# ScalarE's order at the ends of the passes, and the last output tile in two halves, in a kernel of banded attention and a mixture of experts

## The chip, the cores and the metric

The kernel runs on one core of a Trainium2 chip. The metric is the device time of one execution in microseconds (us); the lower the better. The engines of the core are named as in the profile: PE is TensorE's matmuls, PEld its loads of weights, DVE is VectorE, ACT is ScalarE, POOL is GpSimd, SP is SyncE, which issues the DMAs.

## The reference

Attention with a local band and a few global keys makes `x` (3072 rows of 512). Eight experts follow, each a layer of 512 to 1024 with a ReLU and a layer of 1024 to 512, weighted by a matrix `P` of a Sinkhorn iteration, all in float32:

```python
attn_out = _attn_ref(**attn_kwargs)
B, H, S, D = attn_out.shape
x = np.ascontiguousarray(attn_out.transpose(0, 2, 1, 3)).reshape(B * S, H * D)
...
for e in range(E):
    h = np.maximum(x @ w1[e], 0.0)
    ye = h @ w2[e]
    out += P[:, e:e + 1] * ye
```

## The kernel before

**Numbers in two parts.** A float32 operand is held as a high and a low part (`wh` and `wl`, `w2h` and `w2l`, `hh` and `hl`), and each product is three matmuls: high times low, low times high, high times high. The high part of a weight is a cast on ScalarE, the low part a subtraction on GpSimd (`split`, L605 and L606). A matmul therefore waits for both.

**Passes and groups.** After the attention (the first 270 us or so), the 3072 rows are worked on in three blocks of 1024. For each block one pass runs over the weights, in 31 groups of 256 columns of an expert's hidden layer. One group is one step of the loop in `pipeline`:

- Layer one (`layer1_strassen`) by Strassen's scheme: seven products m1 to m7, of six matmuls each, in the order m3, m2, m1, m6, m5, m4, m7, into four banks of PSUM, named c, d, a, b. m3 reads a part of `wh` and `wl` that comes straight from the weights (`w1f`); m2, the second product, reads a part that comes from sums of weights (`wsum`, made on GpSimd, L628). The banks are combined on DVE (L718 to L732; the copy at L716 is the first step), and each is then evicted: ReLU on ACT (L677), then the low part on DVE (L678), into one of two sets of `h` in turn (their names are `h_set` and `x`). When DVE reads a bank, ACT's eviction of that bank waits for this read.
- Layer two (`second`, `layer2`): eight tiles of 128 rows, six matmuls each into a tile `y_ps`, which DVE then adds to the accumulators (L1041, L1045; the buffer is named `early`).

Layer two runs one step behind: layer one of group n, then layer two of group n - 1. At the end of a pass (`p > 0 and g % NG == 0`) both layers two are done before the next pass, so that layer one of the new pass's first two groups follow each other without a layer two between them.

**Weights.** `strassen_stage` loads `w1f` and `w2f` of a group and makes `wsum`; the staging buffers are single. `strassen_pair` makes the high and low parts in this order of the code: the two small ones from `w1f`, then `w2h` from `w2f`, then the big one of five blocks from `wsum`. The results lie in one of two pools, in turn, each with a single buffer: the parts of group n + 2 overwrite those of group n. `w2h` of group n + 2 thus waits until layer two of group n has ended on PE.

**What sets the order.** A scheduler places the instructions on their engines and may put a later one first, except those that are given to `keep_in_program_order`, which stand among themselves in the order of the code. The class `Ordered` wraps an engine in this way. All matmuls of the main loop are kept in order (`moe.pe = attention.pe` once an expert above 0 is reached). `moe.act` is the ScalarE handle for casts and ReLUs: it is wrapped in `Ordered` for the last unit of the attention, and is the bare engine in the main loop, so that the scheduler places casts and evictions there.

**The end.** The last group of a pass also stores each finished tile of the output, 128 rows of 512 columns, from SP's queue (L1048).

## Time and profile before

| what | us |
|---|---|
| runs (3): median, least, most | 2182.03, 2181.88, 2183.47 |
| the profiled execution | 2182.23 |
| its span, from the first instruction to the last | 2180.3 |
| TensorE busy in the span | 2166.7 |
| mean granted TensorE clock, of full speed | 0.999 |

The page of a profile shows one execution. A row of the timeline gives the start in us from the span's start, the length, the engine, the line of the kernel, the operation with output and input, and in brackets the idle time of the engine before it with what ended it. Where a line is that of a wrapper (L110 for all ordered matmuls, L54 for what `Ordered` wraps), the tile's name tells what the instruction is. The chain of waits follows the end of the program back, at each step to what released it. Numbers at the end of a tile's name tell buffers apart in the program's order; the profile leaves them out.

### The profile page before, as it was taken

Reading aid. Unit: us, or ns where it says so; the run is one execution under the profiler, and the core shown is the slowest. Engines: PE = TensorE matmul, PEld = TensorE weight load, DVE = VectorE, ACT = ScalarE, POOL = GpSimd, SP = SyncE. Lnnn points to the kernel's source line nnn. Section 1 sums busy time; section 2 is a strip of 40 time slices with the busy share of each in tenths; the row PEclk is TensorE's granted clock in tenths of the full one; section 3 lists DMA queues with packets and bytes.
Section 4 is the critical chain, followed back from the end, with each engine's and each line's share of the span. In section 5 each row is a group of like instructions: output and inputs, shape, how many; then the busy total and the mean of one; then the engine's idle time right before and its main releaser. Section 6 shows DMA issues by size and latency. Waiting matters only on the chain.

```text
span 2180.3 us, 29188 instructions
## 1 busy us (share of the span) xinstructions
PE 2166.7 (99%) x10785; PEld 1797.7 (82%) x10785; DVE 1375.7 (63%) x2422; ACT 747.4 (34%) x1513; POOL 1153.8 (53%) x1076
## 2 busy tenths in 40 slices
PE   8999999999999999999999999999999999999998
PEld 6888888888888888888888888888888888888887
DVE  7777577566566566566566566566566566566565
ACT  7777633222222232232222232232242232222221
POOL 5977865455454454455454454454455455454440
PEclk9999999999999999999999999999999999999999
DMA  6777531111111111711111111113411111111111
GB/s 164 211 210 205 166 141 58 49 49 59 49 49 58 49 49 59 260 49 58 49 49 58 49 49 58 49 49 127 135 49 58 49 49 58 49 49 58 49 39 51
DMA packets 207881, 175.57 MB, mean 81 GB/s; under 512 B 101232, under 2 KB 170352, under 8 KB 207728
## 3 DMA queue, kind: packets, MB, share of 16 engines
q1 hardware_dynamic: 207728, 173.60, 25.6%
q8 instruction: 87, 1.43, 0.3%
q14 instruction: 66, 0.54, 0.1%
HBM read 144.46 MB, written 29.10 MB: 80 GB/s over the span
## 4 chain that ended last, share of the span: by engine, by line
PE 98%; DVE 1%; DMA 1%; ACT 1%; issue 0%; SPq 0%; DVEq 0%; ACTq 0%
PE y_ps L110 46%; PE bank_a L110 11%; PE bank_d L110 11%; PE bank_c L110 11%; PE bank_b L110 6%; PE t_ps L113 2%; PE o_ps L110 2%; PE s_ps L110 2%; PE h_ps L110 1%; PE tp L113 1%; PE y_ps L748 1%; PE y_ps L746 1%; PE y_ps L747 1%; PE g_ps L110 0%; PE r_ps L113 0%; DMA raw_q<-in_q_dram 0%
## 5 line engine op out<-in xcount | busy, mean ns | idle before, releaser
L1045 DVE SCALAR_TENSOR_TENSOR early<-y_ps,pm,early 128x512 f32<-128x512 f32 x672 | 503.7, 750 | 243.9 <-PE y_ps L110 242.8
L110 PE MATMUL y_ps<-w2h,h_set 128*128 128x512 f32 x1440 | 443.3, 389 | 0.0
L110 PE MATMUL y_ps<-w2h,x 128*128 128x512 f32 x1440 | 443.3, 389 | 0.0
L606 POOL TENSOR_TENSOR wl<-w1f,wh 128x256 fp32r<-128x256 f32 x186 | 134.1, 740 | 561.3 <-ACT wh L605 560.3
L606 POOL TENSOR_TENSOR w2l<-w2f,w2h 128x1024 fp32r<-128x1024 f32 x93 | 222.5, 2393 | 292.7 <-ACT w2h L605 292.7
L628 POOL TENSOR_TENSOR wsum<-w1f 128x256 f32<-128x256 f32 x465 | 327.7, 739 | 84.0 <-DMA w1f<-in_moe_w_dram 84.0
L605 ACT CAST w2h<-w2f 128x1024 fp32r<-128x1024 f32 x92 | 96.9, 1053 | 717.6 <-issue 636.5
L110 PEld LDWEIGHTS y_ps<-w2h,h_set 128*128 128x128 f32 x1440 | 270.3, 188 | 56.1
L110 PEld LDWEIGHTS y_ps<-w2h,x 128*128 128x128 f32 x1440 | 270.3, 188 | 56.1
L110 PE MATMUL y_ps<-w2l,x 128*128 128x512 f32 x720 | 280.1, 389 | 0.0
L110 PE MATMUL y_ps<-w2l,h_set 128*128 128x512 f32 x720 | 280.1, 389 | 0.0
L606 POOL TENSOR_TENSOR wl<-wsum,wh 128x1280 fp32r<-128x1280 f32 x93 | 274.8, 2955 | 3.1
L110 PE MATMUL bank_a<-m,wh 128*128 128x512 f32 x712 | 248.3, 389 | 0.9 <-DVE h_set L678 0.5
L110 PE MATMUL bank_d<-x,wh 128*128 128x512 f32 x712 | 248.2, 389 | 0.0
L110 PE MATMUL bank_c<-x,wh 128*128 128x512 f32 x712 | 248.1, 389 | 0.0
L718 DVE TENSOR_TENSOR early<-early,bank_d 128x512 f32<-128x512 f32 x93 | 64.0, 688 | 187.3 <-PE bank_d L110 177.6
L110 PEld LDWEIGHTS y_ps<-w2l,x 128*128 128x128 f32 x720 | 135.1, 188 | 28.1
L110 PEld LDWEIGHTS y_ps<-w2l,h_set 128*128 128x128 f32 x720 | 135.1, 188 | 28.0
L110 PEld LDWEIGHTS bank_a<-m,wh 128*128 128x128 f32 x712 | 133.6, 188 | 29.5 <-DVE x L678 0.9
L110 PEld LDWEIGHTS bank_c<-x,wh 128*128 128x128 f32 x712 | 133.6, 188 | 27.8
L110 PEld LDWEIGHTS bank_d<-x,wh 128*128 128x128 f32 x712 | 133.6, 188 | 27.7
L110 PE MATMUL bank_a<-m,wl 128*128 128x512 f32 x356 | 138.5, 389 | 0.0
(235 smaller groups left out, 3406.2 us busy)
## 6 DMA issues: line engine op xcount, KB each, us to landing
w1f<-in_moe_w_dram SPq DMA_DIRECT2D x94, 512.0 KB, 3.4
w2f<-in_moe_w_dram SPq DMA_DIRECT2D x94, 512.0 KB, 3.4
x<-op_m SPq DMA_DIRECT2D x16, 512.0 KB, 7.1
op_m<-op SPq DMA_DIRECT2D x30, 256.0 KB, 2.7
m<-op_m SPq DMA_DIRECT2D x12, 512.0 KB, 8.7
out_dram<-early SPq DMA_DIRECT2D x24, 256.0 KB, 4.0
ys<-y_sb SPq DMA_DIRECT2D x21, 256.0 KB, 2.7
early<-ys SPq DMA_DIRECT2D x21, 256.0 KB, 4.5
```

Source lines behind the costliest of these rows:

```text
L110: return self.tc.keep_in_program_order(self.engine.matmul(*args, **kw))
L113: return self.tc.keep_in_program_order(self.engine.transpose(*args, **kw))
L605: self.act.copy(out=hi, in_=full)
L606: self.nc.gpsimd.tensor_tensor(out=lo, in0=full, in1=hi, op=ALU.subtract)
L628: nc.gpsimd.tensor_tensor(out=s[:, n], in0=x, in1=y, op=op)
L718: tt(out=t3, in0=t3, in1=d, op=ALU.subtract)
L746: self.pe.matmul(y_ps, lhsT=hh[:, cols], rhs=lf, start=(f == 0), stop=False)
L747: self.pe.matmul(y_ps, lhsT=hl[:, cols], rhs=wf, start=False, stop=False)
L748: self.pe.matmul(y_ps, lhsT=hh[:, cols], rhs=wf, start=False, stop=(f == n - 1))
L1045: nc.vector.scalar_tensor_tensor(out=a, in0=y_ps, scalar=moe.pm[:, tt, e:e + 1], in1=a, op0=ALU.mult, op1=ALU.add)
```

## The change

There are two parts. First, where a pass ends, ScalarE's handle is wrapped in `Ordered` from ahead of the first group's layer one to the end of the second group's casts, the copy at L716 goes through that handle as well, and the casts of the second group are put ahead of layer one of the first. Second, the last tile of the output is made as two halves of 256 columns, each with its own matmuls, its own step on DVE, and its own store.

```diff
@@ layer1_strassen
         product("m3", "c", True, False)
-        nc.scalar.copy(out=t3, in_=c)
+        self.act.copy(out=t3, in_=c)
         product("m2", "d", True, False)
@@ layer2
-    def layer2(self, t, w, hs, ps, tag):
+    def layer2(self, t, w, hs, ps, tag, out=slice(None)):
         y_ps = ps.tile([P, self.DM], F32, name="y_ps", tag=tag)
         cols = slice(t * P, (t + 1) * P)
         w2h, w2l = w[2:4]
         n = len(hs)
         for f, (hh, hl) in enumerate(hs):
-            wf, lf = (w2h[:, f % FG], w2l[:, f % FG])
-            self.pe.matmul(y_ps, lhsT=hh[:, cols], rhs=lf, start=(f == 0), stop=False)
-            self.pe.matmul(y_ps, lhsT=hl[:, cols], rhs=wf, start=False, stop=False)
-            self.pe.matmul(y_ps, lhsT=hh[:, cols], rhs=wf, start=False, stop=(f == n - 1))
+            wf, lf, y = w2h[:, f % FG, out], w2l[:, f % FG, out], y_ps[:, out]
+            self.pe.matmul(y, lhsT=hh[:, cols], rhs=lf, start=(f == 0), stop=False)
+            self.pe.matmul(y, lhsT=hl[:, cols], rhs=wf, start=False, stop=False)
+            self.pe.matmul(y, lhsT=hh[:, cols], rhs=wf, start=False, stop=(f == n - 1))
         return y_ps
@@ pipeline
-        def second(g, b, hs):
+        def pieces_out(t, w, hs, a, j):
+
+            for cs in (slice(0, DM // 2), slice(DM // 2, DM)):
+                y_ps = moe.layer2(t, w, hs, yps, "y", cs)
+                nc.vector.scalar_tensor_tensor(out=a[:, cs], in0=y_ps[:, cs], scalar=moe.pm[:, j, E - 1:E], in1=a[:, cs],
+                                               op0=ALU.mult, op1=ALU.add)
+                nc.sync.dma_start(out=moe.out[j * P:(j + 1) * P, cs], in_=a[:, cs])
+
+        def second(g, b, hs, last=False):
...
                     j = 2 * t + i
                     tt = b * BT + j
+                    if last and j == BT - 1:
+                        pieces_out(t, wts[g], hs[i], acc[:, j], tt)
+                        continue
...
                 second(*prev)
                 seed(b)
                 prev = None
+
+                moe.act = Ordered(tc, nc.scalar)
+                wts[g + 1] = moe.strassen_pair(moe.strassen_stage(*groups[(g + 1) % NG], stage), wpools[(g + 1) % 2])
             hs = moe.layer1_strassen(ops[p % 2], wts[g], h_sets[n % 2], tmp, mps, "h", n == 0, beat)
             if g + 1 < len(steps) and g + 1 not in wts:
                 wts[g + 1] = moe.strassen_pair(moe.strassen_stage(*groups[(g + 1) % NG], stage), wpools[(g + 1) % 2])
+            if g % NG == 1:
+                moe.act = nc.scalar
...
-        second(*prev)
+        second(*prev, last=True)
```

Call the first four groups of a new pass A, B, C and D. In the program of before their buffers are 9462 and 9464 (A), 9697 to 9700 (B), 9780 to 9783 (C) and 9927 to 9930 (D); in the changed one B's are 9636 to 9639, and the others keep their numbers. A's banks are 9626 and up before, 9648 and up in the changed one; B's are 9709 and up, C's 9856 and up.

On ACT, from B's `w2h` cast to the copy of B's layer one, at the first pass end, before:

```order
L605 CAST w2h_9699<-w2f_9688 128x1024
L716 COPY early_63<-bank_c_9626 128x512
L677 ACTIVATE x00_169<-bank_b_9629 128x512
L677 ACTIVATE x01_170<-bank_d_9627 128x512
L605 CAST wh_9780<-w1f_9770 128x256 x2
L605 CAST wh_9780<-wsum_9774 128x1280
L677 ACTIVATE x00_169<-bank_c_9626 128x512
L677 ACTIVATE x01_170<-bank_a_9628 128x512
L716 COPY early_63<-bank_c_9709 128x512
```

The same stretch in the changed program:

```order
L54 CAST w2h_9638<-w2f_9627 128x1024
L54 CAST wh_9636<-wsum_9630 128x1280
L54 COPY early_63<-bank_c_9648 128x512
L54 ACTIVATE x00_169<-bank_b_9651 128x512
L54 ACTIVATE x00_169<-bank_c_9648 128x512
L54 ACTIVATE x01_170<-bank_d_9649 128x512
L54 ACTIVATE x01_170<-bank_a_9650 128x512
L54 COPY early_63<-bank_c_9709 128x512
```

A's four evictions now follow each other, C's casts are gone from between them, and B's cast of `wsum` has come behind B's cast of `w2h`.

On ACT a layer later, from B's last eviction to C's copy, in the changed program:

```order
L54 ACTIVATE h_set_4963<-bank_a_9711 128x512
L54 CAST wh_9780<-w1f_9770 128x256 x2
L605 CAST wh_9927<-w1f_9917 128x256 x2
L54 CAST w2h_9782<-w2f_9771 128x1024
L54 CAST wh_9780<-wsum_9774 128x1280
L716 COPY early_63<-bank_c_9856 128x512
L605 CAST wh_9927<-wsum_9921 128x1280
L677 ACTIVATE x00_169<-bank_b_9859 128x512
```

C's casts stand here, the one of `wsum` behind the one of `w2h`, and D's cast of `wsum` behind C's copy and ahead of C's first eviction. Before, C's cast of `wsum` stood two layers one earlier, among A's evictions (above).

On POOL, from the low parts of B to those of C, before:

```order
L606 TENSOR_TENSOR w2l_9700<-w2f_9688,w2h_9699 128x1024
L606 TENSOR_TENSOR wl_9781<-w1f_9770,wh_9780 128x256 x2
L606 TENSOR_TENSOR wl_9781<-wsum_9774,wh_9780 128x1280
L628 TENSOR_TENSOR wsum_9921<-w1f_9917 128x256 x5
L606 TENSOR_TENSOR wl_9928<-w1f_9917,wh_9927 128x256 x2
L606 TENSOR_TENSOR wl_9928<-wsum_9921,wh_9927 128x1280
L628 TENSOR_TENSOR wsum_10068<-w1f_10064 128x256 x5
L606 TENSOR_TENSOR w2l_9783<-w2f_9771,w2h_9782 128x1024
```

And in the changed program:

```order
L606 TENSOR_TENSOR w2l_9639<-w2f_9627,w2h_9638 128x1024
L606 TENSOR_TENSOR wl_9637<-wsum_9630,wh_9636 128x1280
L628 TENSOR_TENSOR wsum_9774<-w1f_9770 128x256 x5
L606 TENSOR_TENSOR wl_9781<-w1f_9770,wh_9780 128x256 x2
L606 TENSOR_TENSOR wl_9928<-w1f_9917,wh_9927 128x256 x2
L606 TENSOR_TENSOR w2l_9783<-w2f_9771,w2h_9782 128x1024
L606 TENSOR_TENSOR wl_9781<-wsum_9774,wh_9780 128x1280
L628 TENSOR_TENSOR wsum_9921<-w1f_9917 128x256 x5
```

C's low part of `wsum` stood well ahead of C's `w2l` before; now it stands right behind it, and D's sums behind both. The second pass end has the same orders with other numbers. The order on PE differs only in the last tile.

## The prediction

> **What bounds the kernel now.** I read the page first, then the chain of work that ended last, then, where that chain leaves TensorE, the timelines of the engines there.

> ```profile
> span 2180.3 us, 29188 instructions
> PE 2166.7 (99%) x10785; PEld 1797.7 (82%) x10785; DVE 1375.7 (63%) x2422; ACT 747.4 (34%) x1513; POOL 1153.8 (53%) x1076
> PE 98%; DVE 1%; DMA 1%; ACT 1%; issue 0%; SPq 0%; DVEq 0%; ACTq 0%
> ```

> TensorE (PE) is busy for 99% of the span and carries 98% of the chain. So work that another engine does in its shadow costs nothing, and any time in which PE waits is paid in full. The chain leaves PE at the end of each pass over the weights. Its columns are start, length, and what:

> ```profile
> 916.37 1.37 PE bank_a L110 x6
> 917.74 0.02 issue
> 917.76 1.89 ACT wh L605 x3
> 919.65 0.49 ACT x L677
> 920.14 0.02 issue
> 920.17 0.70 DVE x L678
> 920.87 0.04 issue
> 920.91 1.66 PE bank_a L110 x6
> ...
> 928.01 10.88 PE y_ps L110 x48
> 938.89 1.36 PE bank_c L110 x6
> ```

> I call the first four groups of a new pass A, B, C and D. Here layer one of A ends at 917.74, and layer one of B follows at once, without a layer two between them to give the evictions time. ScalarE (ACT) first makes casts (L605, for C), then evicts A's bank, VectorE (DVE) follows, and only then has PE a free bank. Seven products of 1.36 us are 9.52 us, and B takes 928.01 - 917.74 = 10.27: the loss is **0.75 us**. It happens once more:

> ```profile
> 1549.53 1.38 PE bank_a L110 x6
> ...
> 1561.18 10.88 PE y_ps L110 x48
> ```

> The same sum, 1561.18 - 1550.91 - 9.52, gives 0.75. So the first part of the change can win at most 1.5 us, and the second only what lies behind PE's end.

> **Part one: evictions ahead of casts.** What the order moves is more than the two evictions. ScalarE's whole stretch now stands in the order of the code, and in the code a group's casts are: two small ones, then w2h, then the big one of wsum. Before, the wsum cast of C ran early, beside B:

> ```profile
> 908.29 1.05 ACT L605 CAST w2h<-w2f 128x1024 fp32r<-128x1024 f32 x1 [9.83 <-PE y_ps L110]
> 917.76 0.71 ACT L605 CAST wh<-w1f 128x256 fp32r<-128x256 f32 x2
> 918.38 1.26 ACT L605 CAST wh<-wsum 128x1280 fp32r<-128x1280 f32 x1
> 919.55 0.58 ACT L677 ACTIVATE x<-bank_c 128x512 fp32r<-128x512 f32 x1
> 938.97 1.05 ACT L605 CAST w2h<-w2f 128x1024 fp32r<-128x1024 f32 x1 [7.74 <-issue]
> ```

> The w2h cast writes a buffer which layer two of the group two before still reads, so it waits for PE: B's begins at 908.29, just after layer one of A began (917.74 - 9.52 = 908.22) and so just after PE ended the last pass, and C's at 938.97, 0.08 us after layer two of A ended at 938.89. In the changed order C's wsum cast stands behind this one, and on GpSimd (POOL) its low part stands behind the low part of w2h. But layer one of C begins at that same moment, and its second product (bank_d) reads wsum's high part with its first matmul and the low part with its second:

> ```profile
> 919.73 2.94 POOL L606 TENSOR_TENSOR wl<-wsum,wh 128x1280 fp32r<-128x1280 f32 x1
> 923.29 3.51 POOL L628 TENSOR_TENSOR wsum<-w1f 128x256 f32<-128x256 f32 x5 [0.62 <-DMA w1f<-in_moe_w_dram]
> 940.09 0.39 PE L110 MATMUL bank_d<-x,wh 128*128 128x512 f32 x1
> 940.10 2.39 POOL L606 TENSOR_TENSOR w2l<-w2f,w2h 128x1024 fp32r<-128x1024 f32 x1 [2.59 <-ACT w2h L605]
> 940.32 0.39 PE L110 MATMUL bank_d<-x,wl 128*128 128x512 f32 x1
> ```

> Counted from the start W of C's w2h cast (938.97): the cast ends at W + 1.05, POOL starts 0.08 later (940.10), w2l takes 2.39, a gap of 0.04, wl takes 2.94 to W + 6.50, and PE starts about 0.04 later (920.87 to 920.91): W + 6.54. Before, that matmul started at 940.32 = W + 1.35. PE waits **5.2 us**, at each of two pass ends: **+10.4 us**. Nothing hides it: PE takes its matmuls in order, and has no idle time later to give back. The first matmul of the product comes in the middle, when the wsum cast is done (about W + 2.2), so PE stands still for about 1.1 us and then about 4.1.

> The gain: with evictions first, A's c bank is evicted when DVE's own read of it (L730) is done. In before that read stands at 917.13:

> ```profile
> 917.13 0.69 DVE L730 TENSOR_TENSOR early<-early,bank_c 128x512 f32<-128x512 f32 x1
> ```

> So ACT starts at about 917.86 rather than 919.55, takes 0.6, DVE 0.69, and the bank is free at about 919.2. If B's third product takes it, as now, the loss of 0.75 is gone; if its second does (due 1.2 us after B's start, as C's at 940.09 is after 938.89: 918.94), 0.3 stays; if a later eviction decides, nothing is won. I take the middle one, since products take banks as they come free: **-0.45** each, -0.9 in all, ends 0 and -1.5.

> At nothing I cost: the wsum cast of B, which now waits for w2h at 908.29 (its low part ends near 908.29 + 1.05 + 0.08 + 2.39 + 2.94 = 914.8, due by B's second product at 918.9; less than 4 us later it costs nothing); the copy of A's c bank behind that cast, which ends near 911.2 instead of a microsecond earlier, since DVE's next step needs A's second product too (908.22 + 2 x 1.36 = 910.94) and has another product's 1.36 us before the step after it; wsum of C on POOL ten us later than now, needed only at W; SyncE's load of D's w2f ahead of E's w1f, which waits for POOL longer than the load itself does. Behind C's stall ACT holds the wsum cast of D, for which POOL needs another 3.51 us (until about W + 10.1); C's first eviction stands behind it, due about then, and a few tenths late is covered by the 10.88 us of layer two.

> **The clock after a pause.** Windows of the trace, with TensorE's busy time and instructions first, and the granted clock as the third column from the end:

> ```profile
> 11.77:15.18 3.41, 2.36 (x20) 1.72 (x20) 2.45 (x11) 2.53 (x10) 3.41 (x4) 1.00 0.61 138
> 15.18:18.59 3.41, 3.41 (x20) 3.19 (x21) 2.74 (x12) 3.41 (x16) 3.33 (x5) 0.50 0.76 172
> 2172.40:2175.80 3.40, 2.14 (x10) 1.44 (x8) 1.71 (x3) 0.00 (x0) 0.00 (x0) 1.00 0.55 205
> 2175.80:2179.20 3.40, 0.00 (x0) 0.00 (x0) 0.00 (x0) 0.00 (x0) 0.00 (x0) 1.00 0.27 90
> 2179.30:2180.30 1.00, 0.00 (x0) 0.00 (x0) 0.00 (x0) 0.00 (x0) 0.00 (x0) 0.50 0.02 8
> ```

> The clock halved for just 3.41 us after a stretch of small matmuls with gaps, and again in the first stretch without work at the end; the two falls, 15.18 and about 2179.2, lie 634 steps of 3.413 us apart. [...] **+3.7 us** for both, ends 1.9 and 5.4, and 0 if the clock stays.

> [...]

> **Part two: the last tile in halves.**

> ```profile
> 140.08 1.41 PE g_ps L110 x8
> 15.88 0.62 PE L110 MATMUL s_ps<-kh,ql 64*128 64x256 f32 x2
> 16.09 0.62 PE L110 MATMUL s_ps<-kh,qh 64*128 64x256 f32 x2
> L110 PEld LDWEIGHTS y_ps<-w2h,h_set 128*128 128x128 f32 x1440 | 270.3, 188 | 56.1
> 2174.57 0.75 DVE L1045 SCALAR_TENSOR_TENSOR early<-y_ps,pm,early 128x512 f32<-128x512 f32 x1 [0.61 <-PE y_ps L110]
> L346 DVE CUSTOM_DVE_ANT_1 p_sb<-s_ps,early 128x256 f32<-128x256 f32 x160 | 60.2, 419 | 2.4 <-PE s_ps L110 1.5
> out_dram<-early SPq DMA_DIRECT2D x8, 256.0 KB, 3.4
> op_m<-x SPq DMA_DIRECT2D x16, 128.0 KB, 3.1
> raw_k<-in_k_dram SPq DMA_DIRECT2D x8, 128.0 KB, 2.6
> ```

> Six matmuls of 512 columns (10.88 / 48 = 0.227 each, 1.36) become twelve of 256. Two of 256 follow each other in 0.21, so 0.107 is the least; 0.188, the load of weights, is the most; a line through 0.227 (512) and 1.41 / 8 = 0.176 (384) gives 0.126, which I take: 1.51, or +0.15, ends -0.1 and +0.9. DVE's last step goes from 0.75 to about 0.42: -0.33. The last store lands 3.4 after issue; stores and loads of 128 KB took 2.6 to 3.1: -0.5, ends -0.8 and 0. The first half's step and store lie beside the second half's matmuls. Sum **-0.7**, ends -1.3 and +0.6.

> **The sum** against the profiled execution (2182.23 us, of which the span is 2180.3): 10.4 - 0.9 + 3.7 - 0.7 = +12.5, or 2194.7. The median of the runs, 2182.03, lies 0.2 lower; I forecast **2194.5 us**, 0.6% slower, with its own range from 2192 to 2197.

> **Rivals.** *Pause alone*: PE waits as above, but the clock does not drop, or drops where little work is behind it: 2182.03 + 10.4 - 0.9 - 0.7 = 2190.8. For it: the trace has no pause of this length in the middle of dense work; against it the rows of the clock. *No pause, so no change that can be measured* (a measurement of this kernel tells some 0.2%, 4.4 us, from none): C's w2h cast waits not for PE but only for its place in ACT's queue, runs beside B in the new order, and the wsum parts are ready in time. This decides from 5.2 us on: if the cast starts that much earlier than W, PE never waits, and the time is 2182.03 - 0.9 - 0.7 = 2180.4. For it speaks the releaser "issue" in the row at 938.97; against it that both rows start 0.08 us after PE's last read, and the one at 908.29 names PE. [...]

> **How the numbers follow.** Forecast 0.64, pause alone 0.22, no pause 0.08, longer low clock 0.06. The range 2190.3 to 2197.2 takes in the first two with the ends of their unknown terms and leaves out the others. Faster by over 0.2% (below 2177.7) would need gains that no row offers: 0.01. Within 0.2%: 0.07. Slower: 0.92.

> **What would show it.** Right: in the timeline of after, layer one of each pass's third group shows a single matmul into bank_d, then a pause of about 4 us ended by POOL's wl; the granted clock reads 0.5 for one slot or two around it; PE's last matmul ends 11.5 to 15 us later than now (just before 2174.57); B takes 9.5 to 9.9 us. Wrong: the wl of C ends before bank_d is due, or the clock stays at 1.00 through the pause.

## The result and the profile after

| what | us |
|---|---|
| before, runs beside the changed kernel (6): median, least, most | 2182.31, 2181.88, 2184.69 |
| after, runs (6): median, least, most | 2197.19, 2196.57, 2198.43 |
| ratio, with its 95% interval | 1.0068 [1.0058, 1.0078] |
| profiled execution: before, after | 2182.23, 2197.03 |
| span: before, after | 2180.3, 2194.8 |

The changed kernel is 0.7% slower. It came out 2.7 us above the forecast of 2194.5. It is 0.2 above the range that the forecast gave for itself (2192 to 2197), and 0.01 inside the wider one (2190.3 to 2197.2). Three of the six runs lie above 2197.2, so that the median stayed inside is luck. Against the runs of before beside it the change cost 14.9 us, where 12.5 were forecast.

The page of the changed kernel first, the same rows that were shown of before:

```profile
span 2194.8 us, 29185 instructions
PE 2173.2 (99%) x10791; PEld 1802.2 (82%) x10791; DVE 1374.9 (63%) x2423; ACT 747.8 (34%) x1513; POOL 1154.4 (53%) x1076
PE 98%; DVE 1%; POOL 0%; DMA 0%; ACT 0%; issue 0%; DVEq 0%; SPq 0%
```

The shares don't betray 14.5 us. PE is even busier by 6.5 us: 5.5 of them lie in the layers one of C, where PE is busy for 11.70 and 12.84 us instead of 9.52, since at half clock its matmuls follow each other 0.43 us apart (from 947.35 to 947.78) instead of 0.23 (from 950.04 to 950.27, at full clock). Only POOL's name is new in the chain. The chain of waits that ended last (start, length, what) shows where it comes in; the first pass end, then the second (the last row of each is cut off where the view ends):

```profile
909.02 1.36 PE bank_c L110 x6
...
919.43 0.60 DVE x L678
...
920.08 1.66 PE bank_d L110 x6
...
928.53 10.89 PE y_ps L110 x48
...
939.45 1.06 ACT w2h L54
...
940.58 2.36 POOL w2l L606
942.94 2.85 POOL wl L606
...
945.83 2.15 PE bank_d L110 x5
...
955.68 9.52 PE y_ps L110 x42
```

```profile
1548.64 1.36 PE bank_c L110 x6
...
1568.15 10.89 PE y_ps L110 x48
...
1579.07 1.06 ACT w2h L54
...
1585.45 2.50 PE bank_d L110 x5
...
1596.44 3.63 PE y_ps L110 x16
```

At C the chain leaves PE for ACT's cast of w2h, then POOL's w2l, then POOL's wl, and comes back to PE at 945.83: three steps in a row that before lay beside other work. PE's own timeline has the single matmul in the middle (in brackets the idle time before it and what ended it):

```profile
940.38 0.39 PE L110 MATMUL bank_c<-x,wh 128*128 128x512 f32 x1
941.71 0.49 PE L110 MATMUL bank_d<-x,wh 128*128 128x512 f32 x1 [0.94 <-ACT wh L54]
945.83 0.50 PE L110 MATMUL bank_d<-x,wl 128*128 128x512 f32 x1 [3.62 <-POOL wl L606]
```

And the windows of PE around both pauses (window, length, TensorE's busy time and instructions, granted clock, DMA share, GB/s):

```profile
942.85:946.26 3.41, 0.43 (x2) 1.00 0.49 154
946.26:949.68 3.42, 3.42 (x10) 0.50 0.00 0
1581.15:1584.56 3.41, 0.49 (x1) 1.00 0.24 60
1584.56:1587.97 3.41, 2.52 (x6) 0.50 0.24 94
1587.97:1591.39 3.42, 3.42 (x9) 0.50 0.36 104
```

After the first pause the clock is at half for one window of 3.41 us, after the second for two. The end of the program, of after and of before:

```profile
2167.64 21.84 PE y_ps L110 x102
...
2189.51 0.48 DVE early L1033
```

```profile
2152.78 21.77 PE y_ps L110 x96
```

**Where the 14.5 us of span went.** The first layer one of the second pass (A's) begins at 909.02 instead of 908.22: +0.8, with nothing of the change ahead of it (in the profiled runs below it begins anywhere from 908.2 to 910.6, also where this part of the program is unchanged). B takes 928.53 - 909.02 - 9.52 = 9.99 instead of 10.27, and at the second end 1568.15 - 1548.64 - 9.52 = 9.99 again: -0.56 together. Layer one of C takes 955.68 - 939.42 = 16.26 and 1596.44 - 1579.04 = 17.40 instead of 9.52: +6.74 and +7.88, 14.62 together. In each of these PE's second matmul of bank_d comes 6.38 after W (945.83 - 939.45, 1585.45 - 1579.07) instead of 1.35, which is 5.03; so 10.06 are the pause, and 4.56 what comes behind it, nearly all of it the half clock. From the last layer two to the end it is 2194.8 - 2167.64 = 27.16 instead of 2180.3 - 2152.78 = 27.52: -0.36. The sum is 0.8 - 0.56 + 14.62 - 0.36 = 14.5.

### The profile page after: what moved, and what is told of

Its sections match the earlier page's. It is cut to its first block, busy times and chain, and to the rows that moved or that the text cites. A ratio compares the mean times of both kernels' runs of the same rounds, so it can differ in the third digit from the quotient of the medians.

```text
span 2194.8 us, 29185 instructions
## 1 busy us (share of the span) xinstructions
PE 2173.2 (99%) x10791; PEld 1802.2 (82%) x10791; DVE 1374.9 (63%) x2423; ACT 747.8 (34%) x1513; POOL 1154.4 (53%) x1076
## 4 chain that ended last, share of the span: by engine, by line
PE 98%; DVE 1%; POOL 0%; DMA 0%; ACT 0%; issue 0%; DVEq 0%; SPq 0%
PE y_ps L110 46%; PE bank_d L110 11%; PE bank_a L110 11%; PE bank_c L110 11%; PE bank_b L110 6%; PE o_ps L110 2%; PE s_ps L110 2%; PE t_ps L113 2%; PE h_ps L110 1%; PE tp L113 1%; PE y_ps L748 0%; PE y_ps L746 0%; PE y_ps L747 0%; PE r_ps L113 0%; PE g_ps L110 0%; DMA raw_q<-in_q_dram 0%
## 5 line engine op out<-in xcount | busy, mean ns | idle before, releaser
L110 PE MATMUL y_ps<-w2h,h_set 128*128 128x512 f32 x1444 | 443.5, 388 | 0.0
L110 PE MATMUL y_ps<-w2h,x 128*128 128x512 f32 x1440 | 443.3, 389 | 0.0
L606 POOL TENSOR_TENSOR wl<-w1f,wh 128x256 fp32r<-128x256 f32 x186 | 134.0, 742 | 561.8 <-ACT wh L605 525.3
L606 POOL TENSOR_TENSOR w2l<-w2f,w2h 128x1024 fp32r<-128x1024 f32 x93 | 222.6, 2394 | 310.3 <-ACT w2h L605 287.3
L628 POOL TENSOR_TENSOR wsum<-w1f 128x256 f32<-128x256 f32 x465 | 327.8, 740 | 75.9 <-DMA w1f<-in_moe_w_dram 75.4
L605 ACT CAST w2h<-w2f 128x1024 fp32r<-128x1024 f32 x88 | 92.7, 1053 | 682.8 <-issue 612.8
L110 PEld LDWEIGHTS y_ps<-w2h,h_set 128*128 128x128 f32 x1444 | 270.8, 188 | 56.0
L110 PEld LDWEIGHTS y_ps<-w2h,x 128*128 128x128 f32 x1440 | 270.3, 188 | 56.1
L110 PE MATMUL y_ps<-w2l,h_set 128*128 128x512 f32 (+1 forms) x722 | 280.4, 388 | 0.0
L110 PE MATMUL y_ps<-w2l,x 128*128 128x512 f32 x720 | 280.1, 389 | 0.0
L606 POOL TENSOR_TENSOR wl<-wsum,wh 128x1280 fp32r<-128x1280 f32 x93 | 275.2, 2959 | 7.1 <-ACT wh L605 4.2
L110 PE MATMUL bank_d<-x,wh 128*128 128x512 f32 x712 | 249.9, 392 | 2.2 <-ACT wh L54 1.9
L110 PE MATMUL bank_a<-m,wh 128*128 128x512 f32 x712 | 249.7, 391 | 0.0
L110 PE MATMUL bank_c<-x,wh 128*128 128x512 f32 x712 | 248.1, 389 | 0.0
L110 PEld LDWEIGHTS bank_d<-x,wh 128*128 128x128 f32 x712 | 134.3, 189 | 31.6 <-ACT wh L54 2.7
L110 PEld LDWEIGHTS y_ps<-w2l,h_set 128*128 128x128 f32 x722 | 135.5, 188 | 28.0
L110 PEld LDWEIGHTS y_ps<-w2l,x 128*128 128x128 f32 x720 | 135.2, 188 | 28.0
L110 PEld LDWEIGHTS bank_a<-m,wh 128*128 128x128 f32 x712 | 134.7, 189 | 28.2
L110 PEld LDWEIGHTS bank_c<-x,wh 128*128 128x128 f32 x712 | 133.7, 188 | 27.8
L110 PE MATMUL bank_d<-x,wl 128*128 128x512 f32 x356 | 139.5, 392 | 7.2 <-POOL wl L606 7.2
## 6 DMA issues: line engine op xcount, KB each, us to landing
op_m<-op SPq DMA_DIRECT2D x30, 256.0 KB, 2.6
out_dram<-early SPq DMA_DIRECT2D x23, 256.0 KB, 4.1
ys<-y_sb SPq DMA_DIRECT2D x21, 256.0 KB, 2.9
early<-ys SPq DMA_DIRECT2D x21, 256.0 KB, 4.8
```

The source lines that it names most:

```text
L110: return self.tc.keep_in_program_order(self.engine.matmul(*args, **kw))
L605: self.act.copy(out=hi, in_=full)
L606: self.nc.gpsimd.tensor_tensor(out=lo, in0=full, in1=hi, op=ALU.subtract)
L628: nc.gpsimd.tensor_tensor(out=s[:, n], in0=x, in1=y, op=op)
```

## The experiments

The theory: C's wsum parts come late, since they now queue behind w2h on ACT and behind w2l on POOL; PE waits for them, and its pause halves the clock. The rivals: the ordered evictions themselves hold C up; the clock has nothing to do with the pause; the halves of the last tile cost something. Between them the eight runs decide. Each is compared with runs of before on the same chip (2182.68 in the first four, 2182.85 with those of the last four).

### One part at a time

Part one alone:

```diff
-        second(*prev, last=True)
+        second(*prev)
```

> The first part of the change alone: the order at the pass ends as in the changed kernel, the last output tile whole as before. Theory: the whole loss lies at the pass ends: 2197.2 plus the 0.4 us that the halves won behind TensorE's end in the trace, 2197.6 (2196 to 2199), with two pauses of about 4 us ended by wl. Rival (the halves cost something, by another order of the program or by the stores): 2182 to 2190.

2197.11 us (2195.93 to 2197.97), ratio 1.0064 [1.0047, 1.0081]. The whole loss is in part one.

Part two alone:

```diff
-        self.act.copy(out=t3, in_=c)
+        nc.scalar.copy(out=t3, in_=c)
...
-                moe.act = Ordered(tc, nc.scalar)
-                wts[g + 1] = moe.strassen_pair(moe.strassen_stage(*groups[(g + 1) % NG], stage), wpools[(g + 1) % 2])
...
-            if g % NG == 1:
-                moe.act = nc.scalar
```

> The second part of the change alone: the last output tile in two halves, pass ends as before. Theory: TensorE's twelve matmuls of 256 columns take 0.07 us longer than the six of 512, VectorE's last step takes 0.48 instead of 0.75, the last store lands earlier: about 0.4 us less in all, 2181.9 (2181 to 2182.5), too little for the runs to tell from 2182.3, so the verdict rests on the time from the last layer two's start to the span's end in the trace: 27.5 before, 27.2 expected. Rival (the halves win what the prediction took, 0.7): 26.8.

2182.5 us (2181.88 to 2184.75), ratio 1.0 [0.999, 1.0009]: in the time it can't be seen. In the trace it can; the chain of waits at the end of this kernel:

```profile
2154.58 21.84 PE y_ps L110 x102
...
2176.45 0.48 DVE early L1033
```

Its span is 2181.7, so the tail takes 27.12, against 27.52 before and 27.2 expected. Six more matmuls cost PE 0.07 (21.84 against 21.77), and DVE's last step is 0.27 shorter (0.48 against 0.75). What lies behind it, 2181.7 - (2176.45 + 0.48) = 4.77 against 2180.3 - (2174.57 + 0.75) = 4.98, is the last store: it gave 0.2, not the 0.5 of the prediction.

### The order of the two casts

The changed kernel, but in the ordered stretch wsum is split ahead of w2:

```diff
+        if self.sums_early:
+            self.split(wh[:, 0:5], wl[:, 0:5], s)
         self.split(w2h, w2l, w2f)
-        self.split(wh[:, 0:5], wl[:, 0:5], s)
+        if not self.sums_early:
+            self.split(wh[:, 0:5], wl[:, 0:5], s)
...
-                moe.act = Ordered(tc, nc.scalar)
+                moe.act, moe.sums_early = Ordered(tc, nc.scalar), True
```

> The changed kernel, but in the ordered stretch the cast of wsum stands ahead of the cast of w2h (high and low part), so that C's sums no longer wait for layer two of A to end. Theory (late sums): the pause of 4.1 us in layer one of C and the half clock behind it both go, while the evictions stay in the changed order, so B still takes 9.99 us as in the changed kernel's trace. Time: before 2182.3, less 2 x 0.28 at the pass ends, less 0.4 at the output's end, 2181.3 (2180 to 2182.5); granted clock at 1.00 through both pass ends. Rival (the order of the evictions and of the copy costs the time, not the sums): nearly nothing changes against the changed kernel, 2195 to 2198, with a wait of PE still in layer one of C.

2182.33 us (2181.42 to 2183.62), ratio 0.9999 [0.999, 1.0009]. One swap of two lines takes all of the loss away; everything else of the change is still there. POOL's timeline in this kernel, and its chain of waits:

```profile
931.54 2.96 POOL L606 TENSOR_TENSOR wl<-wsum,wh 128x1280 fp32r<-128x1280 f32 x1
```

```profile
919.49 1.66 PE bank_d L110 x6
...
927.95 10.88 PE y_ps L110 x48
938.83 1.36 PE bank_c L110 x6
940.19 1.36 PE bank_d L110 x6
```

C's wl is made at 931.54 to 934.50, over 4 us before C begins, and in C the product in bank_d follows the one in bank_c at once. The mean granted clock of this execution is 0.999, as before. So the late wsum parts are the cause of the pause, and without the pause the clock didn't fall here. B, behind A's start at 908.43, still takes 10.0 (927.95 - 908.43 - 9.52), as in the changed kernel: that loss has another cause.

### Casts left to the scheduler

The changed kernel, with only the evictions and the copy held in the order of the code:

```diff
-        self.act.copy(out=hi, in_=full)
+        self.cast.copy(out=hi, in_=full)
...
+        moe.cast = moe.act
...
-        moe.act = nc.scalar
+        moe.act = moe.cast = nc.scalar
```

> The changed kernel with only the evictions and the copy of c held in the order of the code, while the casts of the weights go where the scheduler puts them, as before. Theory: it was the casts' place in the order that made C wait, so wsum's parts of C are made beside B as before, the pause at C is gone and the clock stays at 1.00. What is left is the loss at B: C's casts stand between the eviction of b and that of c in ScalarE's queue, and bank_d or bank_a comes free later, by their 1.9 us less what the evictions wait anyway: a loss at B of 1 to 2.1 us instead of 0.75, so 2182.5 - 0.4 + 2 x (0.3 to 1.3) = 2182.7 to 2184.7. Rival (the ordered evictions themselves make C late): a pause of some 5 us stays in C, 2193 or more.

2186.57 us (2184.47 to 2188.16), ratio 1.0018 [1.0008, 1.0027]. ACT's timeline beside B, and the chain:

```profile
917.77 0.72 ACT L605 CAST wh<-w1f 128x256 fp32r<-128x256 f32 x2 [2.75 <-PE bank_a L110]
918.39 1.25 ACT L605 CAST wh<-wsum 128x1280 fp32r<-128x1280 f32 x1
919.55 0.58 ACT L54 ACTIVATE x<-bank_c 128x512 fp32r<-128x512 f32 x1
920.04 0.58 ACT L54 ACTIVATE x<-bank_d 128x512 fp32r<-128x512 f32 x1
```

```profile
916.37 1.38 PE bank_a L110 x6
...
929.41 10.88 PE y_ps L110 x48
940.29 1.36 PE bank_c L110 x6
941.65 1.36 PE bank_d L110 x6
```

No pause at C: the casts stand beside B again, as before. But now B loses 929.41 - 917.75 - 9.52 = 2.14 instead of 0.75 (2.10 at the second end, 1563.93 - 1552.31 - 9.52), because c and d are both evicted behind the casts, while before, the scheduler had put d ahead of them. So the ordered evictions alone don't make C late, and by themselves, without the casts held back, they make B worse. The profiled execution (2184.47) is explained by that: 2182.23 + 1.39 + 1.35 - 0.4 = 2184.57. The other nine runs lie up to 3.7 us higher, above what was expected (2182.7 to 2184.7), and there is no trace of them. The two slowest show a mean granted clock of 0.998 and 0.997 instead of 0.999, but a run of 2186.7 shows 1.000, so a half clock behind B's longer wait may be a part of it and can't be all. That stays open.

### What the pause costs besides itself

The changed kernel, with matmuls put into C's pause (`NIDLE` of them, 18 in one run, 9 in another); nothing reads their result:

```diff
         self.act.copy(out=t3, in_=c)
+        if warm is not None:
+            w_ps = warm.tile([P, WIDE], F32, name="w_ps", tag="s")
+            for m in range(NIDLE):
+                self.pe.matmul(w_ps, lhsT=wh[:, left["m3"], 0], rhs=x["m3"][0][:, :, 0], start=(m == 0), stop=(m == NIDLE - 1))
...
-            hs = moe.layer1_strassen(ops[p % 2], wts[g], h_sets[n % 2], tmp, mps, "h", n == 0, beat)
+            hs = moe.layer1_strassen(ops[p % 2], wts[g], h_sets[n % 2], tmp, mps, "h", n == 0, beat, sps if p > 0 and g % NG == 2 else None)
```

> The changed kernel with 18 more matmuls of 512 columns between the first and second product of layer one of C, into a bank that nothing reads; they take 18 x 0.227 = 4.1 us, in which TensorE stands still in the changed kernel, and so make it no longer. Theory (the pause halves the clock): the granted clock stays at 1.00 at both pass ends, and the 4.6 us that the half clock cost in the profiled execution come back: 2197.2 - 4.6 = 2192.6 (2191 to 2194); the second product still waits for wl, until 6.4 us after the start of C's w2h cast. Rival (the half clock costs nothing, since what is behind the pause would have waited anyway): 2197 as the changed kernel.

2192.83 us (2192.07 to 2193.58), ratio 1.0047 [1.003, 1.0064]: 4.4 less than the changed kernel (and 4.3 less than part one alone, which ran on the same chip), by matmuls that compute nothing. The windows in which the pause ends:

```profile
944.32:947.73 3.41, 2.57 (x12) 1.00 0.23 89
1582.61:1586.02 3.41, 2.71 (x12) 1.00 0.14 53
```

The clock stays at 1.00, at both ends. PE goes on no earlier than in the changed kernel (945.22 - 938.75 and 1583.31 - 1576.84, W + 6.47 at both ends, against 6.38), so the 4.4 us are the half clock, and 10 us the wait. Layer one of C takes 14.73 at both ends of this trace, 0.09 more than 9.52 and the wait of 5.12; so some 0.2 of the 4.56 above are not the clock.

With 9 matmuls instead of 18:

> The changed kernel with 9 extra matmuls of 512 columns, instead of 18, in C's pause; nothing reads their result. At 0.227 us they fill 2.05 us of the 5.03, so PE then stands still for about 2.9 us in one piece (0.23 us of the 5.03 is the lone matmul that reads wsum's high part), and wl still ends the pause at W + 6.38. What is told apart is what halves the clock. Theory 'a slot of 3.41 us that is filled by less than half': 2.9 us without work leave more than 1.7 us of it in one slot in four positions of five, so the clock falls at most pass ends and the time stays near the changed kernel's: 2196 to 2197.5, mean granted clock 0.995 to 0.997. Rival 'only a slot nearly without work' (in the changed kernel the slots ahead of the falls held 0.2 to 0.4 us of work): no slot has less than 0.5 us here, the clock stays, and the time is that of 18 matmuls: 2192.8, clock 0.998 to 1.000. Anything between 2193.5 and 2195.5 would say that one end falls and the other does not.

2193.93 us (2191.61 to 2196.06), ratio 1.0051 [1.0035, 1.0066], neither of the two but between them, and the windows show why:

```profile
942.60:946.02 3.42, 0.59 (x3) 1.00 0.51 153
946.02:949.43 3.41, 3.41 (x9) 0.50 0.00 1
1580.89:1584.30 3.41, 1.76 (x8) 1.00 0.17 24
1584.30:1587.72 3.42, 2.24 (x10) 1.00 0.34 129
```

The same pause, 2.83 us long at both ends by PE's rows, was followed by half clock at one and not at the other, so its length alone doesn't decide. The windows of the second end are steps of 3.413 us counted on from the fall at 946.02 (186 of them to 1580.89). At the first end the pause fell whole into one such step (the slot of 3.41 us in the expectation), which held 0.59 us of work; at the second it was split over two, with 1.76 and 2.24 us.

### A shorter pause

The changed kernel, with wsum's low part ahead of w2's on POOL, and the two held in this order; ACT's order is as it was:

```diff
+        if isinstance(self.act, Ordered) and self.low_first:
+            self.act.copy(out=w2h, in_=w2f)
+            self.act.copy(out=wh[:, 0:5], in_=s)
+            pool = Ordered(self.tc, self.nc.gpsimd)
+            pool.tensor_tensor(out=wl[:, 0:5], in0=s, in1=wh[:, 0:5], op=ALU.subtract)
+            pool.tensor_tensor(out=w2l, in0=w2f, in1=w2h, op=ALU.subtract)
+            return wh, wl, w2h, w2l
```

> The changed kernel, where GpSimd makes wsum's low part before w2's; ScalarE's order stays as it is, w2h first and then wsum. wl then waits for wsum's cast (W + 0.95 start, about 1.3 long, so about W + 2.3) and takes 2.9: it ends at W + 5.2 instead of W + 6.4, and C's pause is 1.2 us shorter at each pass end. Theory (PE waits for wsum's low part and nothing else): the pause is 3.8 to 3.9 us instead of 5.03; the clock still falls, since about 2.9 us without work stay in one piece; 2197.2 - 2.4 = 2194.8, and 1 us more or less by where the slots lie. Rival (w2's low part is needed as early, so that the wait only moves): 2197. If the clock does not fall with this pause: 2190.4.

2193.88 us (2192.99 to 2195.88), ratio 1.005 [1.0034, 1.0065]. Its PE at C, and the windows:

```profile
945.73 0.79 PE L110 MATMUL bank_d<-x,wl 128*128 128x512 f32 x1 [2.46 <-POOL wl L54]
```

```profile
941.60:945.01 3.41, 0.73 (x2) 1.00 0.00 0
945.01:948.42 3.41, 2.69 (x6) 0.50 0.00 0
...
1583.30:1586.71 3.41, 1.28 (x6) 1.00 0.00 0
1586.71:1590.12 3.41, 3.41 (x10) 0.50 0.38 105
```

The idle time ahead of this matmul is 2.46 instead of 3.62, 1.16 less, as expected, and the clock still falls at both ends; two ends of 1.16 are 2.3. The medians differ by 3.3, but the four runs themselves spread over 2.9; in the profiled executions the layers one of C differ by 2.2 (16.35 and 15.10 here, 16.26 and 17.40 there). So PE waited for wsum's low part, and w2's low part, now made behind it, was not needed that early. The window ahead of the second fall held 1.28 us of work, where the rival in the run with 9 matmuls took one nearly without work for granted.

### The version that the runs point to

The swap of the casts, and in the ordered stretch the eviction of d ahead of that of c:

```diff
-        r12 = self.relu_split(c, hs[1])
-        r21 = self.relu_split(d, hs[2])
+        if self.sums_early:
+            r21 = self.relu_split(d, hs[2])
+            r12 = self.relu_split(c, hs[1])
+        else:
+            r12 = self.relu_split(c, hs[1])
+            r21 = self.relu_split(d, hs[2])
```

> The changed kernel with wsum's cast ahead of w2h's (the run that read 2182.33), and in the ordered stretch the evictions in the order b, d, c, a instead of b, c, d, a. At B its PE still loses 0.48 us for each pass end: bank_d's second use waits for VectorE's low part at 918.84 to 919.44, behind the late c. Theory: with d evicted ahead of c, that bank is free by B's second product, and B takes 9.52: 0.75 less than before at each of the two ends, and 0.4 less behind the last layer one: 2182.5 - 1.5 - 0.4 = 2180.6, ratio 0.9991, B 9.5 to 9.6 in the chain of waits. Rival (VectorE's additions into the early tile, ahead of both low parts, decide, and the order of c and d does not): B stays at 10.0, 2181.5 to 2182.4.

2180.71 us (2180.14 to 2182.78, 11 runs), ratio 0.9993 [0.9984, 1.0002]; expected 2180.6. The chain of waits:

```profile
918.00 1.36 PE bank_c L110 x6
919.36 1.36 PE bank_d L110 x6
...
927.52 10.88 PE y_ps L110 x48
```

B takes 927.52 - 918.00 = 9.52: no loss is left, and the chain doesn't leave PE at the pass end (nor at the second, from 1540.88 to 1559.92, which is 2 x 9.52). This does what the change was put there for. It is 16.5 us faster than the changed kernel; of before the trace shows 0.75 less at each end and 0.4 less in the tail, but the interval of the times still holds 1.

## Why the prediction held, and where its sizes were off

**The pause at C was right, step by step.** A single matmul into bank_d, standstill ahead of it and a longer one behind it, ended by wl: the rows show it at 941.71 and 945.83, with 0.94 and 3.62 us idle (forecast about 1.1 and 4.1). Forecast W + 6.54, measured W + 6.38, since w2l took 2.36 instead of 2.39 and wl was done 2.85 after it in place of 2.98 (0.04 and 2.94); 5.03 instead of 5.2 at each end, 10.06 instead of 10.4. The swap of the casts shows the cause. The rival "no pause" falls with the rows. What the prediction put at nothing cost nothing that can be seen: the 14.5 us above are used up without it.

**The clock was right in kind, and too small.** Forecast 3.7 for both ends, with 1.9 and 5.4 as bounds; measured 4.56 in the profile (1.71 and 2.85, with some 0.1 each that isn't the clock), 4.4 as the difference of the medians with 18 matmuls in the pause. The 3.7 and its bounds were the author's estimate of how long the clock stays at half, and no run shows a rule from which they follow; what the runs showed in its place is half clock for one window of 3.41 us or for two. At the second end the first of the two was busy for 2.52 of 3.41 us, and the next was at half all the same. It held six matmuls, where 2.57 us at full clock held twelve (the run with 18 matmuls). Why the clock stayed at half there was not shown. "Pause alone" falls with the windows at 0.50; the run with 18 matmuls, which has the pause without the half clock, is what this rival described, and measured 2192.83 where it gave 2190.8.

**The evictions won less.** Forecast 0.45 at each end (0.3 of the loss left), measured 0.28 (0.47 left). The mechanism that was taken is the one that came: A's c bank is free 1.49 after B's start (919.43 + 0.60 - 918.54; forecast 1.46), and B's second product takes it. That the two agree so well is in part luck: DVE made c's low part behind L732 (918.73, 0.70), a step that the forecast left out, and the low part then took 0.60 in the chain, not 0.69. The term was mis-sized in PE's restart: a product behind a wait takes 1.66 in its row, not 1.36, and the due time of 1.2 that was used holds only part of that: 920.08 + 1.66 - 918.54 - 2 x 1.36 = 0.48. The prediction missed that d can be free earlier than c, although the order of before has d's eviction ahead of C's casts and c's behind them.

**The last tile** gave 0.36 instead of 0.7, nearly all of the difference in the store (0.2 instead of 0.5; the matmuls cost 0.07, not 0.15). The floor of 0.107 us for 256 columns was misread: the rows at 15.88 and 16.09 lie in the window at half clock and hold pairs of matmuls on 64 rows. Here twelve took (1.36 + 0.07) / 12 = 0.119 each.

**Of the 2.7 us** by which the forecast fell short, 0.9 are the clock, 0.3 the evictions and 0.3 the tail, less 0.3 of the pause: 1.2 (13.7 measured for these terms, 12.5 forecast). Another 0.8 is the earlier start of the second pass in the profiled execution of before, with nothing of the change ahead of it. Of the remaining 0.7, 0.3 is time outside the span (2197.03 - 2194.8 against 2182.23 - 2180.3), and about 0.2 each is how far the two profiled executions lie from the medians. The runs of the changed kernel scatter by 1.9 us from the least to the most, so none of these small parts can be seen in the times alone.

## What to carry to other kernels

Who puts one class of instructions into a hand-written order takes over every order among them: before wrapping an engine, list all that stands in the stretch with when each is ready and when it is due; here two casts, not the evictions, decided. A scheduler's odd order can have a reason that a rule ("evictions first") loses: it had put the bank that was free earlier first. On an engine that is busy 99% of the time, a wait of several microseconds can cost more than its length: count the slower clock behind it, here 4.4 us on 10. Behind the short waits at B (0.5 to 2.1 us) the chains of waits show no such loss: the product right behind one takes 1.66 or 1.67 us, those after it 1.36 to 1.38, as at full clock.

## What the runs showed of the hardware

```profile
946.98:950.39 3.41, 2.97 (x7) 0.50 0.14 54
1585.26:1588.68 3.42, 1.89 (x5) 0.50 0.38 140
```

At the end of the changed kernel a step with 0.77 us of work (2188.70 to 2192.11) was followed by a fall.

Of steps with between 1.28 and 1.76 us of work the rows show none, so what follows one was not measured. The busy time alone doesn't tell the two kinds apart: the step at 11.77 before was busy for 2.36 us with small matmuls and was followed by a fall, the one with 2.24 us of large matmuls (the run with 9) was not, and in the changed kernel a step at half clock that was full of small matmuls (3.42 us busy, 14.42 to 17.84) was followed by another at half. Which property of the small ones counts wasn't tried.
